# Loading p once in fp32 and scoring all batches by 32-row pieces in a two-stage attention and token-mixing kernel

## The chip, the cores and the metric

The kernel runs on one core of a Trainium2 chip. The core has a matrix engine (TensorE, PE in the profile), a vector engine (VectorE, DVE), an activation engine (ScalarE, ACT), a general engine (GpSimd, POOL) and a queue engine (SyncE, SP). Each works through its own instruction queue in order; semaphores hold an instruction back until what it needs is there. Sixteen DMA engines move data between HBM and the core's memory (SBUF); results of matmuls land in a second memory (PSUM) of eight banks. SyncE and ScalarE issue DMAs through hardware queues, GpSimd through a software queue; in this kernel the loads that cast fp32 to bf16 are all issued by GpSimd. The metric is device time in microseconds, as the median of several runs.

## What is computed

All inputs are fp32. There are 8 batches, 8 heads, 576 positions and a head size of 64; p has 32 packed positions per head.

```python
def sm_attn(qq, kk, vv):
    s = scale * np.matmul(qq, kk.transpose(0, 1, 3, 2))
    a = softmax(s)                      # over the last axis
    return np.matmul(a, vv)

p_packed = sm_attn(p, k, v)             # first attention: 32 x 576 scores per head
attn     = sm_attn(q, p_packed, p_packed)   # second attention: 576 x 32 scores per head
x   = attn.transpose(0, 2, 1, 3).reshape(8, 576, 512)
wq, wk = x @ w_q, x @ w_k               # 512 -> 64 each
mixed  = (wq @ wk.T / 8) @ x            # per batch
out    = np.maximum(mixed, 0) @ w_out   # 512 -> 512
```

## The kernel before

The program is one long list of steps, the string ORDER, that is read from left to right; each item issues the instructions of one step. `S1.3=2,3,6,7` is step S1 for batch 3 with PSUM banks 2, 3, 6 and 7; `X2.1.2@A` is step X2 for batch 1, part 2, on ScalarE (`@V` is VectorE, `@P` GpSimd, `@S` SyncE). So the order of each engine's queue is written out by hand, and batches overlap as the list interleaves them. A step waits only for what it needs, but it also waits for all that stands ahead of it in its engine's queue.

One batch goes through these steps:

- LD.k, LD.v, LD.q: loads, issued by GpSimd with a cast to bf16 (`load`, L153 to L185). Buffers for four batches (NL = 4) take turns. Half of k of batch 0 comes in fp32 by SyncE (LD.H) and is cast by ScalarE (HC).
- KT turns k by 32 x 32 blocks on VectorE (L242, `blocks`), S1 multiplies it with p on PE, X1 takes the exponential on ScalarE. In batches 2 to 7 S1 works by pieces of 32 rows (32 matmuls, L288) straight from pT, the turned p; X1 then comes in two parts (L299) and TE turns the result back (two VectorE instructions). In batches of DIAG (0 and 1) S1 works with a block-diagonal copy of p, `pblk` (36 matmuls, L278), X1 is one instruction (L296), and TE is not needed.
- PV multiplies with v (L321); RC and PP divide by the row sums (L325, L329); PT turns the packed result; QK multiplies it with the projection weights (L342), QKE and QD copy that out.
- QV turns q; S2 scores q against the packed result (L379), X2 takes the exponential (L384), RS and RR sum and invert (L400, L405), AM multiplies (L411) on VectorE or GpSimd; AT turns the result on PE (L420, L425), AE copies it out.
- WKQ, WE, GM, GE, Y, YE, MX, MR, RL, RLR are the token mixing up to the ReLU (L447 to L511); OT multiplies with the output weights (L546), OE and OEF copy out, ST and STF store.

p reaches the core twice: LD.E0 (ScalarE's queue) and LD.E1 (SyncE's) fetch batches 0 and 1 in fp32 with rows of 256 bytes, EC casts them on ScalarE, EX turns them, and four PB copies put them into `pblk`, which SET.pz0 has zeroed. LD.P0 to LD.P3 fetch all of p with a cast through GpSimd's queue, and PX turns it into pT later.

WARM items are filler: matmuls on a constant tile whose results nobody reads (L621). `WARM.15=3` is 15 units of 128 columns, in matmuls of 512 columns if not said otherwise (`WARM.16.128` is 16 units in matmuls of 128). Each shows as two instructions in the profile. HOLD.v7 is a tiny DMA on SyncE that reads the last v buffer, so that the stores behind it in SyncE's queue start only when that load has landed.

GpSimd's loads share eight completion semaphores in turn, so the issue of a load waits until the load eight places earlier has landed.

Of the kernel before, what the change touches and what calls it, by code (L numbers as in the profile page):

```python
# [7 lines left out]
NL, NB, NO, NE = 4, 3, 6, 2  # L8
DIAG = (0,1)
# [7 lines left out]
SET.v1@P S2.0.0=2,3 X2.0.0@A LD.v1 LD.P0 WARM.8=4 QK.0=4 RR.0.1@V AM.0.1@V QKE.0@A LD.q1 RS.0.0@V SET.aff@P  # L17
SET.idb@V WARM.3=5 S1.1=0,1,2 X1.1.0@A WARM.6=5 PV.1.0=4,5 PV.1.1 X2.0.2@A RR.0.0@V AT.0.1=3 AM.0.0@V AT.0.0=2
AE.0.0@A RC.1@V PP.1.1@V RS.0.2@V RR.0.2@V AM.0.2@V AE.0.1@A QD.0@A WARM.5=0 WKQ.0.0=0,1 AT.0.2=5 LD.k2
AE.0.2@A WARM.1=6 WKQ.0.2 LD.v2 WE.0.0@A WKQ.0.1 LD.q2 LD.k3 WE.0.1@A WARM.3=6 GM.0=5 PP.1.0@V PT.1@V QK.1=4  # L20
QV.1.2@V S2.1.1=6,7 GE.0@A S2.1.0=2,3 LD.O PX@V S2.1.2=0,1 KT.2.2@V QKE.1@A X2.1.1@A RS.1.1@V X2.1.0@A Y.0=4,5
YE.0@A WARM.1=6 S1.2=6,7,2,3 X2.1.2@A LD.v3 RS.1.0@V MX.0.1=4,5 RR.1.1@V X1.2.0@A TE.2.0@V X1.2.1@A TE.2.1@V
RR.1.0@V WARM.7=0 PV.2.0=0,1 PV.2.1 RL.0.1@A RS.1.2@V AM.1.0@V QD.1@A MR.0=6,7 RLR.0@A LD.k4 RR.1.2@V
MX.0.0=2,3 LD.q3 RC.2@V AT.1.0=4 AM.1.2@V AT.1.2=5 AE.1.2@A RL.0.0@A PP.2.1@V AM.1.1@P AT.1.1=6 AE.1.1@A
PP.2.0@V AE.1.0@V WARM.2=7 WKQ.1.0=0,1 WKQ.1.2 WARM.2=7 WKQ.1.1 QV.2.2@V WE.1.0@A PT.2@V S2.2.3=4,5 S2.2.2=2,3
KT.3.2@V WE.1.1@A GM.1=7 QK.2=6 GE.1@V WARM.3=0 Y.1=0,1 X2.2.2@A QKE.2@V S1.3=2,3,6,7 X2.2.3@A RS.2.4@V
RR.2.4@V LD.v4 X1.3.1@A TE.3.1@V X1.3.0@A TE.3.0@V OT.0.0=4,5 OT.0.1 LD.q4 YE.1@A AM.2.2@V OT.0.2=6,7 OE.0.0@V
OT.0.3 MR.1=2,3 OE.0.1@A RLR.1@V MX.1.1=0,1 PV.3.0=4,5 PV.3.1 RL.1.1@A RC.3@V PP.3.1@V PP.3.0@V KT.4.2@V
AM.2.3@P QD.2@P AT.2.3=2 AE.2.3@A OT.1.4=3 MX.1.0=6,7 AT.2.2=5 OEF.1.4@A AE.2.2@V WKQ.2.0=0,1 PT.3@V QV.3.2@V
WKQ.2.1 RL.1.0@A WKQ.2.2 WE.2.2@A S1.4=2,3,4,5 X1.4.1@A X1.4.0@A TE.4.1@V OT.1.0=6,7 LD.k5 GM.2=0 QK.3=1  # L30
QKE.3@A S2.3.2=4,5 X2.3.2@A S2.3.3=2,3 X2.3.3@A GE.2@V Y.2=0,1 OT.1.1 OE.1.0@A TE.4.0@V YE.2@V PV.4.0=4,5
PV.4.1 MX.2.0=0,1 RL.2.0@A RS.3.4@V LD.v5 RR.3.4@V RC.4@V LD.q5 PP.4.1@V PP.4.0@V PT.4@V OT.1.2=2,3 OT.1.3
QK.4=6 QV.4.2@V MX.2.1=0,1 MR.2=4,5 OE.1.1@A RL.2.1@A RLR.2@V AM.3.3@P QKE.4@V AT.3.3=7 AE.3.3@V QD.3@P
# [26 lines left out]
def kernel(  # L60
# [27 lines left out]
    P = 128  # L88
# [50 lines left out]
    def quarter(x):  # L139
        return slice(x * 32, (x + 1) * 32)  # L140
# [12 lines left out]
    def load(x, eng):  # L153
# [3 lines left out]
        elif a == "P":  # L157
            c = int(b)
            src = p.rearrange("b (i c) (y l) d -> c (b i) y (l d)", i=2, y=2)
            nc.gpsimd.dma_start(pbf[quarter(c)], src[c])  # L160
        elif a == "E":
            b = int(b)
            src = p[b].rearrange("(i c) l d -> (c l) i d", i=2)
            (nc.sync if eng == "S" else nc.scalar).dma_start(p32[:, 2 * b:2 * b + 2], src)
        elif a == "W":
            w = (moe_w_k, moe_w_q)[int(b)].rearrange("(i c j e) m -> (c j) i (e m)", i=2, c=4, e=2)
            nc.gpsimd.dma_start(wqk[:, :, int(b)].rearrange("a i e m -> a i (e m)"), w)
        elif a == "O":
            nc.gpsimd.dma_start(wout, moe_w_out.rearrange("(j a) n -> a j n", a=P))
        elif a == "H":  # L170
# [73 lines left out]
    def EC(eng, bk):  # L244
        copy(eng, pbe, p32.rearrange("a u d -> a (u d)"))
# [409 lines left out]
```

## Time and profile before

| | |
|---|---|
| median of 3 runs | 106.0 us (105.98 to 106.29) |
| profiled execution, whole | 105.18 us |
| its span, first to last instruction | 103.3 us |
| PE busy | 96.8 us, 94% of the span |
| PE weight loads | 58.4 us |
| VectorE busy | 75.7 us |
| ScalarE busy | 66.2 us |
| GpSimd busy | 49.9 us |
| bytes written by DMA | 25.16 MB |
| mean granted TensorE clock | 0.991 |

The busy time of PE includes the filler matmuls: 76 instructions of L621, 23.6 us with overlaps. The profile shows, for each group of instructions, its line, engine, operation and tiles, its count, its total and mean time, and what ended the idle time ahead of it. The chain of waits is followed back from the last instruction, at each step to what released it. A timeline row gives the start in us, the time in us, the engine, the line, the operation and in brackets the idle time before it. A row of a stretch of time (A:B) gives its length, then busy time and count of instructions of PE, PE weight loads, VectorE, ScalarE and GpSimd, the granted clock, the DMA engines' busy share, and GB/s written.

### The profile page before, as it was taken

To read this page: it belongs to the slowest core of one execution; us is meant where nothing else is said; L and a number is where in the kernel's file an instruction comes from. 1 tells how busy PE (TensorE), PEld (TensorE's weight loads), DVE (VectorE), ACT (ScalarE), POOL (GpSimd) and SP (SyncE) were. 2 spreads that over 40 slices of the span, in tenths; PEclk is the share of its full clock that TensorE was granted. 3 is DMA by queue.
4 is the path that set the end of the run, shared out by engine and by line. 5 is a ranking of instruction groups with operands and counts; after the bars stand their busy time and mean duration, and the time that the engine had idled before them with its cause. 6 is when DMAs were issued, how large, how long until landed. Compare 5 with 4: busy or idle time off the path is not lost.

```text
span 103.3 us, 3603 instructions
## 1 busy us (share of the span) xinstructions
PE 96.8 (94%) x1544; PEld 58.4 (57%) x1544; DVE 75.7 (73%) x150; ACT 66.2 (64%) x109; POOL 49.9 (48%) x76
## 2 busy tenths in 40 slices
PE   5999999999999999799999999999999999999950
PEld 3897545766756654456636655683567654744430
DVE  5072381969989899798699979989988999526310
ACT  5142104246896954779869869899898695659440
POOL 5779882962263316930049689506589129000000
PEclk9999999999999999999999999999999999999996
DMA  2999999999999999999999999999999999999884
GB/s 71 262 149 191 209 208 198 210 211 213 204 213 212 203 208 213 212 206 211 211 210 208 220 208 203 215 211 207 209 259 377 402 410 400 403 409 366 341 305 164
DMA packets 14079, 25.16 MB, mean 244 GB/s; under 512 B 2160, under 2 KB 7024, under 8 KB 14064
## 3 DMA queue, kind: packets, MB, share of 16 engines
q0 software_dynamic: 10448, 16.88, 85.1%
q1 hardware_dynamic: 3200, 7.87, 19.9%
q8 instruction: 12, 0.20, 0.7%
q10 hardware_dynamic: 416, 0.20, 0.7%
q14 instruction: 3, 0.02, 0.1%
HBM read 30.28 MB, written 9.44 MB: 384 GB/s over the span
## 4 chain that ended last, share of the span: by engine, by line
PE 73%; DVE 9%; DMA 5%; ACT 5%; POOL 3%; issue 2%; DVEq 0%; POOLq 0%; ACTq 0%
PE ps L546 25%; PE ps L621 13%; PE ps L321 6%; DMA k_sb<-in_k_dram 5%; PE ps L379 5%; PE ps L452 4%; PE ps L498 4%; PE ps L425 4%; DVE rs L400 3%; ACT e L384 3%; PE ps L447 3%; PE ps L278 2%; PE ps L473 2%; PE ps L288 2%; PE ps L342 2%; POOL a L411 2%
## 5 line engine op out<-in xcount | busy, mean ns | idle before, releaser
L546 PE MATMUL ps<-wout,relu 128*128 128x512 bf16 x124 | 30.5, 380 | 0.0
L411 POOL TENSOR_TENSOR a<-e,rr 128x1024 bf16<-128x1024 f32 (+2 forms) x13 | 15.6, 1211 | 19.1 <-DVE rr L405 11.0
L621 PE MATMUL ps<-o 128*128 128x128 f32 (+3 forms) x76 | 23.6, 452 | 1.3 <-DVE o L134 1.2
L127 ACT ACTIVATE o<-ps 128x1024 f32<-128x1024 f32 (+2 forms) x17 | 15.0, 888 | 6.9 <-PE ps L546 6.3
L546 PEld LDWEIGHTS <-relu 128*128 128x128 bf16 x124 | 10.7, 98 | 12.3 <-issue 1.8
L621 PEld LDWEIGHTS ps<-o 128*128 128x128 f32 x76 | 12.7, 220 | 7.1 <-issue 4.9
L384 ACT ACTIVATE e<-ps 128x256 f32<-128x256 f32 (+2 forms) x19 | 11.3, 621 | 5.9 <-PE ps L379 5.5
L509 ACT ACTIVATE relu<-ps 128x1024 bf16<-128x1024 f32 (+1 forms) x14 | 12.7, 933 | 2.2 <-PE ps L498 1.1
L242 DVE STREAM_TRANSPOSE kT<-k_sb 128x1152 uint32<-128x1152 uint32 (+1 forms) x9 | 11.1, 1232 | 3.0 <-DMA k_sb<-in_k_dram 2.9
L176 POOL DMA_DIRECT2D v_sb<-in_v_dram x16 | 10.1, 637 | 6.4 <-PE ps L425 2.1
L242 DVE STREAM_TRANSPOSE qT<-q_sb 128x1152 uint32<-128x1152 uint32 (+1 forms) x10 | 11.2, 1119 | 0.7 <-DMA q_sb<-in_q_dram 0.7
L400 DVE TENSOR_REDUCE rs<-e 128x16 f32<-128x512 f32 (+2 forms) x13 | 10.9, 846 | 0.5 <-ACT e L384 0.4
L321 PE MATMUL ps<-v_sb,e 64*64 64x192 bf16 x288 | 7.5, 245 | 0.7 <-DVE o L131 0.7
L299 ACT ACTIVATE e1T<-ps 128x576 bf16<-128x576 f32 x12 | 7.2, 663 | 1.3 <-PE ps L288 1.2
L127 ACT ACTIVATE aT<-ps 128x128 bf16<-128x128 f32 (+2 forms) x11 | 5.3, 506 | 3.6 <-PE ps L425 2.1
L321 PEld LDWEIGHTS <-e 64*64 64x64 bf16 x288 | 6.0, 107 | 2.6 <-issue 0.9
L127 ACT ACTIVATE wkq<-ps 128x448 bf16<-128x448 f32 (+1 forms) x9 | 6.3, 713 | 1.7 <-PE ps L452 1.4
L452 PE MATMUL ps<-aT,pqk 128*128 128x256 bf16 (+1 forms) x48 | 6.8, 246 | 0.1
L379 PEld LDWEIGHTS <-qT 64*128 64x128 bf16 x320 | 5.5, 94 | 2.3 <-issue 0.7
L379 PE MATMUL ps<-ppT,qT 64*128 64x64 bf16 x320 | 6.6, 190 | 0.0
L179 POOL DMA_DIRECT2D k_sb<-in_k_dram x7 | 5.2, 745 | 2.7 <-ACT g L127 2.7
L447 PE MATMUL ps<-pqk,aT 128*128 128x64 bf16 x80 | 6.1, 194 | 0.1
(80 smaller groups left out, 143.2 us busy)
## 6 DMA issues: line engine op xcount, KB each, us to landing
v_sb<-in_v_dram POOLq DMA_DIRECT2D x16, 288.0 KB, 11.5
out_dram<-o SPq DMA_DIRECT2D x9, 512.0 KB, 6.6
k_sb<-in_k_dram POOLq DMA_DIRECT2D x7, 576.0 KB, 11.9
q_sb<-in_q_dram POOLq DMA_DIRECT2D x6, 576.0 KB, 15.4
out_dram<-o POOLq DMA_DIRECT2D x4, 512.0 KB, 7.4
out_dram<-o SPq DMA_DIRECT2D x5, 256.0 KB, 2.7
q_sb<-in_q_dram POOLq DMA_DIRECT2D x4, 288.0 KB, 9.7
out_dram<-orem SPq DMA_DIRECT2D x4, 256.0 KB, 5.7
```

The source lines that it names most:

```text
L127: nc.scalar.activation(o, i, COPY)
L176: nc.gpsimd.dma_start(v_bufs[b % NL][halves(i), 0:7:2], src)
L242: nc.vector.transpose(o, i)
L321: nc.tensor.matmul(T["pv", b][halves(cc), i], lhsT, rhs, start=n == 0, stop=n == R - 1, skip_group_check=True)
L379: nc.tensor.matmul(ps[:, y, t - t0, i], lhsT, rhs, start=e == 0, stop=e == 1)
L384: nc.scalar.activation(e2[:, t0:t1].rearrange("a t (i y n) -> a y (t i) n", i=2, y=2), T["s2", b, c].rearrange("a y t i n -> a y (t i) n") ...
L400: nc.vector.tensor_reduce(rs[:, t0 * H:t1 * H], src, axis=AX, op=ADD)
L411: e.tensor_tensor(a2[:, t0:t1].rearrange("a t i (u l) -> a (t i u) l", l=L), e2v(b, c), T["rr", b][:, t0 * H:t1 * H].to_broadcast((P, (t1 ...
L452: nc.tensor.matmul(o, pqk[:, i, Dl:], aT[:, i, c0:c1], start=i == 0, stop=i == 1)
L509: nc.scalar.activation(o, i, RELU)
L546: nc.tensor.matmul(ps, lhsT, wout[:, j, :], start=j == 0, stop=j == NJ - 1)
L621: nc.tensor.matmul(bank(int(bk), [w]), warm[:, 0:P], rhs, start=True, stop=True)
```

## The change

- LD.E0, LD.E1 and LD.P0 to LD.P3 are gone. One load, LD.N, brings all of p in fp32 by ScalarE's hardware queue, in 128 rows of 4 KB. NC casts it in two halves, one on ScalarE, one on VectorE, and PX turns each half into pT, all before the first score step. EC, EX, the four PB copies and SET.pz0 are gone.
- DIAG is empty: S1, X1 and TE of batches 0 and 1 work as in the others, by pieces.
- The order of all steps, their engines and their banks is new. All 19 AM steps and all 8 QD steps are on GpSimd (13 and 4 before). The loads behind p and k come as g (half of k of batch 0), v0, r0 and q0 (halves of q), the two projection weights, k1, k2, v1, q1, v2, q2, k3, output weights, k4, v3, q3, v4, q4, k5, q5, v5, k6, v6, q6, k7, r7, v7, q7; before, k7, v7, r7, q7 stood last, and the four loads of p stood among the first ones. The filler is 81 units instead of 82. One store moves from GpSimd to SyncE, behind HOLD.

```diff
-DIAG = (0,1)
+DIAG = ()
...
-SET.warm@V SET.v3@V SET.pz0@V LD.E0@A SET.tab@A SET.aT1@V LD.H@S LD.P3 LD.E1@S EC@A EX@V PB.0.1@V LD.g0
-SET.v0@P HC@A PB.0.3@V PB.0.2@V KT.0.0@V KT.0.1@V LD.v0 PB.0.0@P WARM.4=0 WARM.16.128=0 S1.0=0,1,2 X1.0.0@A WARM.6=3
-PV.0.0=4,5 PV.0.1 RC.0@V LD.q0 SET.mask@P SET.idf@V SET.aT0@V QV.0.1@V PP.0.0@V LD.P2 LD.r0 PP.0.1@V PT.0@V
-SET.v2@V LD.W0 QV.0.0@V WARM.15=3 S2.0.2=6,7 LD.k1 LD.W1 SET.aT2@V LD.P1 KT.1.2@V S2.0.1=0,1 X2.0.1@A RS.0.1@V
...
+LD.H@S SET.warm@V SET.v0@V SET.aT0@V SET.aT1@V SET.aT2@V SET.idf@V LD.N@A SET.tab@A LD.g0 NC.0@A NC.1@V PX.1@V
+PX.0@V HC@A KT.0.0@V KT.0.1@V LD.v0 LD.r0 LD.q0 LD.W0 LD.W1 LD.k1 SET.mask@P SET.aff@P SET.idb@V WARM.4=0
+WARM.17.128=0 S1.0=0,1,2,3 X1.0.0@A TE.0.0@V X1.0.1@A TE.0.1@V WARM.8=4 PV.0.0=4,5 PV.0.1 RC.0@V PP.0.0@V
+PP.0.1@V PT.0@V QV.0.0@V QV.0.1@V WARM.12=6 S2.0.2=6,7 X2.0.2@A RS.0.2@V RR.0.2@V LD.k2 S2.0.0=0,1 X2.0.0@A
+S2.0.1=2,3 RS.0.0@V RR.0.0@V X2.0.1@A SET.v1@P LD.v1 LD.q1 RS.0.1@V SET.v2@P RR.0.1@V LD.v2 QK.0=4 QKE.0@A
+AM.0.2@P WARM.5=5 AT.0.2=5 AE.0.2@A AM.0.0@P WARM.5=6 AT.0.0=6 KT.1.2@V WARM.2=7 S1.1=0,1,2,3 AM.0.1@P
+AT.0.1=7 AE.0.0@V QD.0@P WKQ.0.0=4,5 WKQ.0.2 SET.v3@P X1.1.0@A LD.q2 LD.k3 WE.0.0@A LD.O AE.0.1@V KT.2.2@V
+LD.k4 WKQ.0.1 X1.1.1@A TE.1.1@V WARM.3=6 S1.2=0,1,6,7 LD.v3 WE.0.1@A GM.0=4 TE.1.0@V GE.0@A X1.2.0@A WARM.1=2
...
@@ load
-        elif a == "P":
-            c = int(b)
-            src = p.rearrange("b (i c) (y l) d -> c (b i) y (l d)", i=2, y=2)
-            nc.gpsimd.dma_start(pbf[quarter(c)], src[c])
-        elif a == "E":
-            b = int(b)
-            src = p[b].rearrange("(i c) l d -> (c l) i d", i=2)
-            (nc.sync if eng == "S" else nc.scalar).dma_start(p32[:, 2 * b:2 * b + 2], src)
+        elif a == "N":
+            src = p.rearrange("b (i c) (y l) d -> (c y) (b i) (l d)", i=2, y=2)
+            (nc.sync if eng == "S" else nc.scalar).dma_start(p32, src)
...
-    p32 = T["o"][NO - 1].rearrange("a t n -> a (t n)")[:, 0:4 * Dh].rearrange("a (u d) -> a u d", u=4)
+    p32 = T["o"][NO - 1].rearrange("a t n -> a (t n)")[:, 0:L * Dh // 2]
...
-    def EC(eng, bk):
-        copy(eng, pbe, p32.rearrange("a u d -> a (u d)"))
+    def NC(x, eng, bk):
+        n = L * Dh // 4
+        copy(eng, pbf[:, x * n:(x + 1) * n], p32[:, x * n:(x + 1) * n])
...
-    def EX(eng, bk):
-        blocks(pe.rearrange("a u l e -> a (u l e)").bitcast(u32), pbe.bitcast(u32))
-    def PX(eng, bk):
-        blocks(pT.rearrange("a u (y l) e -> a (u y l e)", y=2).bitcast(u32).rearrange("a (u l) -> a l u", l=L // 2),
-               pbf.bitcast(u32).rearrange("a (l n) -> a l n", l=L // 2))
+    def PX(x, eng, bk):
+        ls = slice(x * L // 4, (x + 1) * L // 4)
+        blocks(pT.rearrange("a u l e -> a (u l e)").bitcast(u32)
+               .rearrange("a (u y l) -> a l y u", y=2, l=L // 2)[:, ls],
+               pbf.bitcast(u32).rearrange("a (l y u) -> a l y u", l=L // 2, y=2)[:, ls])
```

More of the change, by code (lines that the diff above doesn't have):

```diff
@@ L17 @@
[L17 to L21, printed above, removed]
@@ new lines @@
+PV.2.0=6,7 PV.2.1 AM.1.2@P AT.1.2=0 AE.1.2@A RC.2@V AM.1.0@P WARM.4=1 AT.1.0=1 AE.1.0@A RR.1.1@V AM.1.1@P
+PP.2.1@V PP.2.0@V PT.2@V WARM.3=2 AT.1.1=2 QK.2=3 QV.2.2@V AE.1.1@A WKQ.1.0=4,5 QKE.2@V WKQ.1.2 WE.1.0@A LD.v4
+WKQ.1.1 WE.1.1@V S2.2.3=6,7 X2.2.3@A S2.2.2=0,1 GM.1=2 X2.2.2@A KT.3.2@V RS.2.4@V RR.2.4@V GE.1@A WARM.4=3
+Y.1=4,5 YE.1@A S1.3=6,7,0,1 X1.3.1@A MX.1.1=2,3 MX.1.0=4,5 OT.0.2=0,1 OT.0.3 X1.3.0@A RL.1.0@A OT.0.0=6,7
+RL.1.1@A TE.3.1@V OE.0.1@A AM.2.3@P AT.2.3=4 OT.0.1 KT.4.2@V AE.2.3@A TE.3.0@V AM.2.2@P AT.2.2=5 AE.2.2@A
@@ new lines @@
+HOLD.v7 ST.2.0@P ST.2.1@P RR.6.4@V AM.6.3@P X1.7.0@A OT.4.2=0,1 OT.4.3 TE.7.1@V MR.4=2,3 ST.0.0 QV.7.0@V
+QK.6=6 WE.5.2@A AM.6.2@P TE.7.0@V RLR.4@V OE.4.1@A GM.5=7 QV.7.1@V AT.6.3=4 AT.6.2=5 AE.6.2@V GE.5@A Y.5=2,3
+ST.1.4 QKE.6@A QD.6@P PV.7.0=0,1 PV.7.1 YE.5@V MR.5=6,7 MX.5.1=2,3 AE.6.3@A WKQ.6.0=4,5 WKQ.6.2 ST.3.4 RLR.5@A
+RC.7@V PP.7.1@V RL.5.1@A WKQ.6.1 PP.7.0@V ST.3.0 PT.7@V MX.5.0=6,7 RL.5.0@V ST.4.0 S2.7.0=0,1 OT.5.4=2
+OEF.5.4@V WE.6.2@A GM.6=3 ST.3.1@P S2.7.2=4,5 X2.7.0@A GE.6@A RS.7.0@V X2.7.2@A RS.7.2@V S2.7.1=0,1 X2.7.1@A
@@ L596, in STF @@
         q.dma_start(orows(b)[:, :, t * D:(t + 1) * D], T["o", b][:, t])
-    steps = dict(EC=EC, HC=HC, EX=EX, PX=PX, PB=PB, KT=KT, S1=S1, X1=X1, TE=TE, PV=PV, RC=RC, PP=PP,
+    steps = dict(NC=NC, HC=HC, PX=PX, PB=PB, KT=KT, S1=S1, X1=X1, TE=TE, PV=PV, RC=RC, PP=PP,
                  PT=PT, QK=QK, QKE=QKE, QD=QD, QV=QV, S2=S2, X2=X2, HA=HA, RS=RS, RR=RR, AM=AM,
```

63 lines of the change are left out of this document (26 added, 37 removed).

## The prediction

> **What bounds the kernel now.** I read the page's slices first.
>
> ```profile
> span 103.3 us, 3603 instructions
> PE   5999999999999999799999999999999999999950
> DMA  2999999999999999999999999999999999999884
> GB/s 71 262 149 191 209 208 198 210 211 213 204 213 212 203 208 213 212 206 211 211 210 208 220 208 203 215 211 207 209 259 377 402 410 400 403 409 366 341 305 164
> HBM read 30.28 MB, written 9.44 MB: 384 GB/s over the span
> ```
>
> Two resources are full almost from the first slice to the last: TensorE (PE) and the DMA engines. GB/s counts bytes written, so a load that casts fp32 to bf16 shows half of what it reads: the level of 210 up to slice 29 is 420 read, the same rate as the 400 of the fp32 stores behind it. The second view is the chain of waits, in order of time.
>
> ```profile
> 2.03 5.55 DMA k_sb<-in_k_dram
> ...
> 8.44 1.23 PE ps L278 x35
> 9.67 1.49 PE ps L621 x4
> 11.16 0.87 PE ps L321 x36
> 12.02 3.42 PE ps L621 x8
> ...
> 19.26 1.16 PE ps L278 x31
> ...
> 40.24 1.66 DVE a L411
> 41.89 1.14 DVE o L131
> ...
> 43.08 0.94 PE ps L321 x36
> ...
> 46.71 0.41 PE ps L288 x20
> ```
>
> Up to 8.4 us it is loads and transposes. From there PE's queue runs nearly without a gap, but not all of it is work: L621 are filler matmuls (WARM), which PE must finish before its next real step. The order has 82 units of filler (a unit is 128 columns), 20 of them ahead of the first score step. Behind 43.08 the chain is PE but for a few detours, to 99.5 (PE is busy for 4.47 us of the stretch from 95 on that is shown further down). So the end is: start of the first score step, plus PE's queue (work and filler), plus its stalls, and the transfers must keep up.
>
> **The change, part by part.** The sum is made against the profiled execution (105.18 us, span 103.3, so 1.88 outside the span); the median of the runs, 106.0, lies 0.82 above it.
>
> *Scores of batches 0 and 1.* Gone are two diagonal score steps of 36 matmuls, 1.23 and 1.16 us on the chain; in their place come two piece steps of 32, which the chain has at 0.41 (46.71 above) and, for batch 2 at 29.03, at 0.47. Gain 2.39 - 2 x 0.44 = **1.5 us** of PE queue; bounds 1.45 and 1.57.
>
> *Filler.* 82 units become 81, 21 of them ahead of the first score step, so 60 instead of 62 behind it. Fifteen units took 3.42 us (12.02), 0.228 each: **0.46 us** less. The extra unit ahead of the first score is one of the narrow ones; the row for 16 narrow and 4 wide ones is 6.98 us, so it adds some 0.4 and PE is free for the first score at about 8.18 + 0.4 = 8.58.
>
> *The start.* Before, ScalarE casts batch 0 and 1 of p, then the first half of k; VectorE turns both:
>
> ```profile
> o<-in_k_dram SPq DMA_DIRECT2D x1, 576.0 KB, 3.6
> 0.75 0.39 SPq L171 DMA_DIRECT2D o<-in_k_dram  x1
> 1.20 6.98 PE L621 MATMUL ps<-o 128*128 128x512 f32 x34 [1.20 <-DVE o L134]
> 4.90 0.42 ACT L127 ACTIVATE o<-o 128x256 bf16<-128x256 f32 x1 [2.16 <-DMA o<-in_p_dram]
> 5.22 1.15 ACT L127 ACTIVATE k_sb<-o 128x1152 bf16<-128x1152 f32 x1
> 5.73 0.44 POOL L129 COPY o<-o 32x256 bf16<-32x256 bf16 x1 [1.00 <-DVE o L242]
> 7.61 0.78 DVE L242 STREAM_TRANSPOSE kT<-k_sb 128x576 uint32<-128x576 uint32 x1 [0.32 <-DMA k_sb<-in_k_dram]
> L242 DVE STREAM_TRANSPOSE pT<-o 128x512 uint32<-128x512 uint32 x1 | 1.0, 1010 | 0.0
> 1.00:2.00 1.00, 0.80 (x1) 0.50 (x2) 0.88 (x3) 0.75 (x1) 0.67 (x1) 1.00 0.33 51
> 2.00:3.00 1.00, 1.00 (x2) 0.34 (x1) 0.37 (x3) 0.73 (x2) 1.00 (x3) 1.00 0.67 264
> 3.00:4.00 1.00, 1.00 (x6) 0.93 (x5) 0.00 (x0) 0.00 (x0) 0.70 (x2) 1.00 1.06 359
> 4.00:5.00 1.00, 1.00 (x7) 1.00 (x7) 0.00 (x0) 0.10 (x1) 0.72 (x2) 1.00 1.10 166
> 5.00:8.00 3.00, 3.00 (x24) 2.98 (x23) 2.24 (x6) 1.37 (x2) 2.10 (x8) 1.00 0.96 152
> ```
>
> The last piece of p, queued behind half of k on SyncE, was there at 4.90: 0.72 MB of fp32 by hardware queues. Now 0.52 MB of p and 0.59 MB of k go together, 0.39 MB more. At 359 per us that is 1.1 us for the pair; p is the smaller of the two and I place its landing at 5.3. Bounds: 4.35, if only k's half is shared with (issue 0.75 plus the 3.6 us to landing in its row), and 6.7, if p, and both halves of k share in thirds (1.57 MB, of which 0.67 by 4.0, the rest at 332 read). From there: p's ScalarE half, 512 columns, lies between 0.42 (256) and 1.15 (1152), about 0.63; k's cast 1.15; two turns of 0.78; hand-overs 0.1. First score at 5.3 + 3.44 = 8.75 against 8.44: **+0.3**, bounds +0.14 (filler) and +1.7. Queued behind the new wait for p on ScalarE stands k's cast, and for it wait the turn of k on VectorE and PE, even where k itself has long landed. VectorE's cast of the other half of p and the two turns into pT (1.01 us for the whole in its row) lie beside ScalarE's 1.78 and cost nothing; were that cover gone, it would be some 1.5. k's other half is issued 0.7 us earlier on GpSimd, since it is first in its queue now, and is wanted only at 7.9.
>
> *Softmax of batch 0.* One exponential becomes two with two turns.
>
> ```profile
> L299 ACT ACTIVATE e1T<-ps 128x576 bf16<-128x576 f32 x12 | 7.2, 663 | 1.3 <-PE ps L288 1.2
> L242 DVE STREAM_TRANSPOSE e<-e1T 128x288 uint32<-128x288 uint32 x12 | 5.4, 463 | 0.9 <-ACT e1T L299 0.7
> L411 POOL TENSOR_TENSOR a<-e,rr 128x512 bf16<-128x512 f32 x3 | 3.1, 1041 | 4.6 <-DVE rr L405 4.6
> L411 DVE TENSOR_TENSOR a<-e,rr 128x512 bf16<-128x512 f32 x3 | 2.1, 687 | 0.1
> ```
>
> Score to p-times-v was 11.16 - 8.44 = 2.72; now 0.47 + 2 x 0.66 + 0.46 and hand-overs, 2.4. It is covered by eight units of filler (1.8) either way: **0**; without them it would be 0.3 gained.
>
> *Normalising (AM) moves to GpSimd*, all 19 of them; six of them ran on VectorE. Each costs 0.35 more (1041 against 687 ns). So do the four copies of pqk (QD) that ScalarE and VectorE had; the rest of the queue behind each is loads. Beside fillers of 5, 5 and 2 units in batch 0 and 4, 4 and 3 in batch 1 most is hidden; I take **+0.5**, bounds 0 and 6 x 0.35 = 2.1.
>
> One stall goes. At 40.16 VectorE's AM on 256 columns took 1.73 us, where its likes at 24.08 and 32.56 took 0.43 and 0.41, and ended 0.3 us behind GpSimd's AM of batch 2:
>
> ```profile
> 39.70 1.90 POOL L411 TENSOR_TENSOR a<-e,rr 128x1024 bf16<-128x1024 f32 x1 [3.11 <-DVE rr L405]
> 40.16 1.73 DVE L411 TENSOR_TENSOR a<-e,rr 128x256 bf16<-128x256 f32 x1
> PE ps L321 <- DVE o L131: 0.7, 1, 0.7
> ```
>
> VectorE's next instruction let PE idle 0.7 us before 43.08. With no AM on VectorE the pair can't meet: **-0.7**, bounds -0.7 and 0 (late next: the 0.6 us AM queued behind the first on GpSimd). The Trainium skill, SBUF — State Buffer, section "SBUF: two separate sides", says that GpSimd and a VectorE instruction with two SBUF inputs lock each other out of a shared port for the whole instruction. The trace agrees (1.73 for 0.43). By that rule alone the next VectorE instruction would come 1.3 us sooner, of which the sum takes 0.7.
>
> PE's side: +0.3 - 1.5 - 0.46 + 0.5 - 0.7 = **-1.9 us**.
>
> *Transfers.* Two small loads of p (0.13 MB, 256-byte rows) go and none is added: 0.3 us at 420 read per us. The full loads are issued earlier, since GpSimd's queue is no longer held by a block copy (5.73) and by four loads of p; the low stretch 5 to 8 us (152 where 209 is usual) has 0.8 us to give. At the end:
>
> ```profile
> 90.00:95.00 5.00, 5.00 (x48) 2.29 (x45) 2.02 (x4) 3.80 (x7) 0.00 (x0) 1.00 0.97 385
> 95.00:101.00 6.00, 4.47 (x25) 2.23 (x23) 1.86 (x4) 2.85 (x6) 0.00 (x0) 1.00 0.88 334
> ```
>
> From 90 to 101 us 3.93 MB were written; at 405 this takes 9.7, so 1.3 us of slack. In all the transfers could end 2.4 us earlier if no gap were left, hardly more than PE's 1.9. Stores on SyncE wait (HOLD) for the last v, which now follows one half of q instead of preceding both; as loads or stores fill the engines then either way, I count nothing for it, nor for the one GpSimd store that moves to SyncE behind HOLD. I take **+0.4** back, bounds 0 and 1.6 (all of PE's 1.9 but the 0.3 of bytes). Sum -1.5: span 101.8, this execution 103.7, median 106.0 - 1.5 = **104.5**. Its own range is 103.5 to 105.4, set by the start and the AM.
>
> **The rivals.**
>
> *p comes late.* Three streams share in thirds, p lands at 6.7 and the first score starts at 10.15, 1.4 later than in the sum: -0.5, **105.5**. For it: all three are issued within 0.6 us. Against it: in the rows up to 5.00 all queues wrote 0.84 MB, 0.72 of it the hardware queues', so GpSimd's loads had moved 0.12. The Trainium skill, DMA: Bandwidth & Descriptors, "Queues, rings and completion order", has each DMA engine serve its rings in turn, a packet each. By that rule p would land with k; the trace bears it out only weakly.
>
> *The transfers bind.* PE gets 1.9 us ahead and then waits for loads or for stores, so only the 0.3 us of bytes remains: **105.7**. For it: 384 GB/s over the span. Against it: from 44 us on no load stands on the chain.
>
> *GpSimd's queue holds the AMs, and it gets slower.* GpSimd issues the loads too, and an issue waits there for an older load to land:
>
> ```profile
> wqk<-in_moe_w_k_dram POOLq DMA_DIRECT2D x1, 64.0 KB, 5.9
> 18.15 1.25 POOL L176 DMA_DIRECT2D v_sb<-in_v_dram  x2 [2.01 <-DMA k_sb<-in_k_dram]
> 24.55 0.62 POOL L176 DMA_DIRECT2D v_sb<-in_v_dram  x1 [1.71 <-DMA q_sb<-in_q_dram]
> ```
>
> In the new order the AMs of batch 0 stand behind the loads k2, v1, q1, v2, those of batch 1 behind q2, k3, the output weights, k4, v3, q3, those of batch 3 behind q5, v5, k6, v6. Behind each AM stands PE, which turns its result next. Two waits of 2.0 and 1.7 that reach the AMs in full cost 3.7: -1.9 + 3.7 = +1.8, **107.8**; it decides from 1.9 us on. For it: both rows fall in a stretch in which VectorE still did all AMs, so before they held back no AM. Against it: the last wait ahead of batch 0's AMs is for the first weight load, 5.9 us to landing in its row; by the durations of the issues ahead of it (0.56 to 1.24) it is issued some 4 us earlier than at 8.57 before, and no AM is wanted before p times v (to 12.0) and twelve filler units (2.7) are over.
>
> **How the numbers follow.** Forecast 0.55; p late 0.12; transfers bind 0.12; GpSimd's queue 0.21. About 0.3%, 0.3 us, is what can be told from no change. Faster: 0.53 of the forecast, 0.07 of late p, 0.06 of the transfers, together 0.66; the same: 0.02, 0.03 and 0.06, 0.11; slower: all of GpSimd's 0.21 and 0.02 of late p, 0.23. The range reaches from the forecast's low end, 103.4, into the GpSimd case, 107.0; above it stays half of that case, 0.1, and below it 0.08.
>
> **What would show it.** The first L281 matmul (the new file's line of the piece scores) at 8.6 to 9.0, with k's cast right behind p's; late p shows as ScalarE waiting on in_p beyond 6. AM of batch 0 with a VectorE reciprocal as its releaser: right; with a DMA issue just in front: the GpSimd rival. PE's last matmul near 97.6 instead of 99.5, and DMA share above 0.95 to the end, confirm the sum with its take-back. Wrong it is if PE gains fillers' worth of new idle time in 12 to 36 us, or waits there on k, q or v.

## The result, and the profile after

The change makes the kernel slower: 111.27 us median (110.54 to 112.02, 5 runs) against 106.0 (105.92 to 107.06), ratio 1.048 [1.041, 1.055]. The forecast was 104.5, in a range up to 107.0. The execution profiled after took 111.63 us, its span 109.9. Ratios, here and below, leave disturbed (slow) runs out, so that they can differ from the quotient of two medians.

First the slices of the page of the changed kernel:

```profile
span 109.9 us, 3565 instructions
...
PE   5980199999999999999989998996999999999950
PEclk9999557999999999999999999999999999999999
DMA  3699999999999999999999999999899955996695
GB/s 119 216 180 181 193 203 211 210 204 192 176 211 204 205 208 206 210 199 188 211 212 205 213 210 208 212 212 205 163 370 390 362 215 212 406 407 252 273 378 178
...
HBM read 30.15 MB, written 9.44 MB: 360 GB/s over the span
```

A slice is 2.75 us. TensorE idles in the fourth and most of the fifth (digits 0 and 1), and its granted clock is about half in the fifth and sixth, where it was full before. At the end the stores no longer fill the engines (215, 212, 252, 273 where 410, 400, 366, 341 stood before): outputs come late. The chain of waits (start, time, what) says what the idle time waits for:

```profile
0.74 9.95 DMA o<-in_p_dram
...
10.71 0.63 ACT o L127
11.34 1.06 ACT k_sb L127
...
12.42 1.45 DVE kT L235 x2
...
13.92 0.70 PE ps L281 x25
14.62 3.67 PE ps L614 x4
18.29 0.87 PE ps L314 x36
19.16 2.77 PE ps L614 x6
21.93 0.71 PE ps L372 x40
```

The single load of p lands at 10.7 us, and everything up to the first score hangs on it: first score 13.92 (8.44 before), p times v 18.29 (11.16), first second-stage score 21.93 (15.44). Of the 7.1 us by which p times v is late, the first score already has 5.5. The rest is the clock: the first scores and the eight units of filler behind them take 0.70 + 3.67 us here, and 0.47 + 1.92 at full clock (in the flat load's kernel below). That is 2.0 more, less the 0.3 by which the piece scores are shorter than the old ones. At the second stage 6.5 us are left, since three units of filler fewer stand in between. From there to the end of the span it is 109.9 - 21.93 = 88.0, before 103.3 - 15.44 = 87.9: the late start goes through to the end, and of what the change was to gain behind this point nothing shows in this kernel.

The stretches around it (PE, PE loads, VectorE, ScalarE and GpSimd busy with counts, clock, DMA share, GB/s written):

```profile
3.00:4.00 1.00, 1.00 (x6) 0.94 (x5) 0.00 (x0) 0.49 (x2) 1.00 (x3) 1.00 0.75 288
4.00:5.00 1.00, 1.00 (x9) 1.00 (x9) 0.00 (x0) 0.00 (x0) 1.00 (x2) 1.00 0.54 137
...
7.00:8.00 1.00, 0.69 (x7) 0.50 (x5) 0.00 (x0) 0.00 (x0) 0.65 (x4) 1.00 1.08 195
8.00:9.00 1.00, 0.00 (x0) 0.00 (x0) 0.00 (x0) 0.00 (x0) 0.00 (x0) 1.00 1.54 164
...
11.00:11.29 0.29, 0.00 (x0) 0.00 (x0) 0.26 (x2) 0.29 (x2) 0.00 (x0) 1.00 1.16 207
11.29:12.00 0.71, 0.00 (x0) 0.00 (x0) 0.71 (x2) 0.71 (x2) 0.68 (x1) 0.50 1.16 209
12.00:13.00 1.00, 0.00 (x0) 0.10 (x1) 0.82 (x2) 0.39 (x1) 0.70 (x3) 0.50 1.29 174
```

Two things stand there. Between 4 and 5 us the DMA engines are half idle although p is outstanding. And PE is empty from 7.7 us on; 3.6 us later, at 11.29, the clock falls in one step from full to half. The trace has it back at full at 18.12.

### The profile page after: what moved, and what is told of

The parts are those of the page before. It is cut to its first block, busy times and chain, and to the rows that moved or that the text cites. A ratio compares the mean times of both kernels' runs of the same rounds, so it can differ in the third digit from the quotient of the medians.

```text
span 109.9 us, 3565 instructions
## 1 busy us (share of the span) xinstructions
PE 95.5 (87%) x1519; PEld 56.1 (51%) x1534; DVE 71.6 (65%) x139; ACT 66.8 (61%) x112; POOL 53.2 (48%) x81
## 3 DMA queue, kind: packets, MB, share of 16 engines
HBM read 30.15 MB, written 9.44 MB: 360 GB/s over the span
## 4 chain that ended last, share of the span: by engine, by line
PE 69%; DMA 9%; DVE 9%; ACT 5%; issue 3%; POOL 2%; DVEq 0%; ACTq 0%; POOLq 0%
PE ps L539 24%; PE ps L614 13%; DMA o<-in_p_dram 9%; PE ps L314 5%; PE ps L372 5%; PE ps L418 4%; PE ps L281 3%; PE ps L445 3%; DVE kT L235 3%; PE ps L491 2%; PE ps L440 2%; PE ps L466 2%; POOL a L404 2%; ACT e L377 2%; PE ps L335 2%
## 5 line engine op out<-in xcount | busy, mean ns | idle before, releaser
L404 POOL TENSOR_TENSOR a<-e,rr 128x256 bf16<-128x256 f32 (+2 forms) x19 | 20.4, 1090 | 23.7 <-DVE rr L398 23.6
L539 PE MATMUL ps<-wout,relu 128*128 128x512 bf16 x112 | 29.2, 380 | 1.1 <-issue 0.5
L614 PE MATMUL ps<-o 128*128 128x128 f32 (+3 forms) x74 | 24.2, 468 | 1.3 <-DVE o L134 1.2
L127 ACT ACTIVATE o<-ps 128x1024 f32<-128x1024 f32 (+1 forms) x16 | 14.3, 892 | 4.2 <-PE ps L539 4.0
L614 PEld LDWEIGHTS ps<-o 128*128 128x128 f32 x74 | 12.0, 216 | 6.9 <-issue 4.9
L292 ACT ACTIVATE e1T<-ps 128x576 bf16<-128x576 f32 x16 | 9.7, 650 | 5.3 <-PE ps L281 5.1
L502 ACT ACTIVATE relu<-ps 128x1024 bf16<-128x1024 f32 (+1 forms) x13 | 12.1, 960 | 0.4 <-PE ps L497 0.3
L171 POOL DMA_DIRECT2D v_sb<-in_v_dram x16 | 10.1, 643 | 1.4 <-POOL v_sb L204 0.7
L281 PE MATMUL ps<-kT,pT 32*32 32x288 bf16 x256 | 4.5, 307 | 5.9 <-DVE kT L235 5.8
L235 DVE STREAM_TRANSPOSE e<-e1T 128x288 uint32<-128x288 uint32 x16 | 7.1, 454 | 1.9 <-ACT e1T L292 1.7
L131 DVE COPY o<-ps 128x1024 f32<-128x1024 f32 (+1 forms) x4 | 3.3, 822 | 5.4 <-PE ps L576 3.5
```

The source lines that it names most:

```text
L127: nc.scalar.activation(o, i, COPY)
L171: nc.gpsimd.dma_start(v_bufs[b % NL][halves(i), 0:7:2], src)
L235: nc.vector.transpose(o, i)
L292: nc.scalar.activation(e1T[:, x], T["s1", b][x].rearrange("a c m -> a m c"), EXP, scale=scale)
L404: e.tensor_tensor(a2[:, t0:t1].rearrange("a t i (u l) -> a (t i u) l", l=L), e2v(b, c), T["rr", b][:, t0 * H:t1 * H].to_broadcast((P, (t1 ...
L502: nc.scalar.activation(o, i, RELU)
```

## The experiments

Three theories stood against each other: the shape of the load (A), the company of GpSimd's loads (B), the ScalarE queue (C); with them, what the lost clock costs. A time without a ratio is that of a single run, unless a median is named.

### The same bytes in another shape

```diff
-            src = p.rearrange("b (i c) (y l) d -> (c y) (b i) (l d)", i=2, y=2)
+            src = p.rearrange("b h (y l) d -> (b h y) (l d)", y=2)
```

> The load of p reads its 128 rows of 4 KB in the order in which they lie in HBM (one outer dimension of 128 in the source instead of 8 by 16); bytes, row size, queue and all else stay. The rows land on other partitions, so the scores are taken with permuted rows of p and the output differs from the reference. Theory A (the load is given to only as many DMA engines as its outermost source dimension of 8 allows, so half of the 16 engines carry p beside their share of the other loads): with 128 it is spread over all, p lands by 6.0 us instead of 10.7, the first score starts by 9.4, PE does not lose its clock, and the time is 104 to 107 us. Theory B (p shares with the many loads that GpSimd now issues early, whatever its shape): p still lands behind 9 us and the time stays within 1 us of 111.3.

Measured: 104.76 us (104.59 to 104.85) against 106.11, ratio 0.990 [0.986, 0.994]. Its chain:

```profile
0.75 5.88 DMA o<-in_p_dram
...
9.86 0.47 PE ps L281 x19
10.33 1.92 PE ps L614 x4
12.25 0.87 PE ps L314 x36
13.12 2.77 PE ps L614 x6
15.89 0.71 PE ps L372 x40
```

The same 128 rows of 4 KB, by the same queue beside the same company, land 4.1 us earlier (at 6.6, where theory A had 6.0), and the kernel is 6.5 us faster. Its stretches from 3 to 5 us:

```profile
3.00:4.00 1.00, 1.00 (x6) 0.94 (x5) 0.00 (x0) 0.00 (x0) 1.00 (x3) 1.00 0.90 344
4.00:5.00 1.00, 1.00 (x7) 1.00 (x7) 0.00 (x0) 0.00 (x0) 1.00 (x2) 1.00 1.01 402
```

Where the changed kernel wrote 137 GB/s at half share, this one writes 402 at a full one. The issue took 0.40 us instead of 1.23. The queues' packets tell why; first the changed kernel, then this one, then one in which p goes by another queue (below):

```profile
q10 hardware_dynamic: 280, 0.66, 2.6%
```

```profile
q10 hardware_dynamic: 288, 0.66, 2.2%
```

```profile
q10 hardware_dynamic: 144, 0.13, 0.3%
```

Without p that queue has 144 packets, so the load has 136 in the first case and 144 in the second: 128 rows plus 8, and 128 rows plus 16. In the trace the extra packets have 4 bytes each, and the semaphore of p's load is raised 8 times between 9.69 and 10.69 us in the changed kernel, 16 times between 5.43 and 6.63 here. I read them as one completion for each DMA engine that takes part: 8 engines for the change's load, 16 for the flat one. The Trainium skill, DMA: Bandwidth & Descriptors, section "Why a DMA increments its semaphore by 16 and not by 1", gives the rule: a DMA is spread over the largest number up to 16 that divides the slowest dimension of both its patterns. The change's source has 8 there, (c y), the flat one 128; the trace agrees (8 and 16 packets).

The edit changes more than the number of engines: the rows come in the order of HBM, the issue is shorter, and p starts sooner. In the trace p's first row moves at 1.99 us here, beside those of k, whose last starts at 5.77. In the changed kernel it moves at 3.33, when k is nearly done (its last row starts at 3.63). GpSimd's first row moves at 4.9 to 5.0 in both kernels. By 5.0 us 410 of the flat load's 524 KB were written, and 229 of the change's.

### GpSimd's loads held back

Casting the second half of p on GpSimd holds every load behind it in that queue until p has landed. In the first of two kernels, GpSimd's half of k of batch 0 goes ahead of this, in the second it too stands behind.

```diff
-LD.N@A SET.tab@A LD.g0 NC.0@A NC.1@V PX.1@V
+LD.N@A SET.tab@A LD.g0 NC.0@A NC.1@P PX.1@V
```

> The cast of p's second half moves from VectorE to GpSimd, where it stands in front of all loads but the first half-load of k, so these are issued only when p has landed. p's access pattern keeps its outer 8. Theory A (half the engines, each with 64 KB of p beside k): p lands at 6 to 7.5, sooner than 10.7 as fewer loads share, but behind the 5.3 forecast. Theory B (sharing alone): p lands at 4.6 to 5.6. In both the later loads come some 4 us later than before; the time is no test.

Measured: 110.5 us; p lands at 9.35, later than either theory had placed it (7.5 at the latest).

```diff
-LD.N@A SET.tab@A LD.g0 NC.0@A NC.1@V PX.1@V
+LD.N@A SET.tab@A NC.0@A NC.1@P LD.g0 PX.1@V
```

> The changed kernel with all of GpSimd's loads behind p: the cast of p's second half moves to GpSimd and stands in front of them. Until p is there only p and SyncE's half of k are under way, so the rates written in this time are theirs. Theory A (half the engines carry p): once k's half has landed (about 4 us) p alone is written at 200 GB/s or less, half of the 400 that the stores reach, and it lands at 5.5 to 7.0. With all engines p would land by 4.7.

Measured: 111.75 us; p lands at 8.44, behind the 5.5 to 7.0 expected, while the rate came as expected, under 200 GB/s. From the chain and the stretches of this second kernel, in which only SyncE's half of k goes with p:

```profile
0.73 7.70 DMA o<-in_p_dram
```

```profile
5.00:6.00 1.00, 1.00 (x11) 1.00 (x10) 0.00 (x0) 0.00 (x0) 0.00 (x0) 1.00 0.49 119
6.00:7.00 1.00, 1.00 (x11) 1.00 (x10) 0.00 (x0) 0.00 (x0) 0.00 (x0) 1.00 0.53 131
```

With p alone in flight the engines are 0.49 to 0.53 busy and write 119 to 131 GB/s. Half of them, then, and less than a third of the 402 GB/s of the flat load's kernel (k and p together). GpSimd's loads together cost 10.7 - 8.4 = 2.3 us. So A and B both hold, and without B it would still be 8.4. But half the engines would explain half the rate, not a third: for the same busy share less was written too, 131 at 0.53, so 247 at a full one, against 398. Four loads on 16 engines, tried below without GpSimd's loads, show the same while p alone is in flight:

```profile
4.00:5.00 1.00, 1.00 (x7) 1.00 (x7) 0.00 (x0) 0.00 (x0) 0.00 (x0) 1.00 0.94 270
```

That is 287 at a full share, so this part doesn't come from the number of engines. Both kernels read rows that lie apart in HBM, the flat load reads them in order; this difference was not tried by itself.

Neither kernel gains more than 0.8 us in time: all later loads start late.

### The other hardware queue

```diff
-LD.H@S SET.warm@V ... SET.idf@V LD.N@A SET.tab@A LD.g0
+LD.N@S LD.H@S SET.warm@V ... SET.idf@V SET.tab@A LD.g0
```

> The same load of p is issued by SyncE ahead of its half of k instead of by ScalarE. Theory C (ScalarE's queue is late or slow: its issue took 1.23 us): p lands more than 2 us sooner than 10.7 and k's half stays near 4.4. Theories A and B: p lands within 1.5 us of 10.7, as shape and sharing are the same.

Measured: 114.5 us. p lands at 9.36 on SyncE's queue, 1.3 us sooner, and the half of k behind it only at 13.9 (the chain has it as 12.27 us of DMA from 1.63 on). C, which asked for more than 2 us, falls; and the load issued second in time is now the starved one.

### More filler ahead of the first score

```diff
-WARM.17.128=0 S1.0=0,1,2,3
+WARM.33.128=0 S1.0=0,1,2,3
```

> Sixteen more narrow filler units ahead of the first score, so that PE stays busy until p is there. If the idle stretch from 7.7 to 13.3 us cost PE its clock, the granted clock stays at 1.0, the eight filler units behind the first score take 1.8 instead of 3.7 us, p times v of batch 0 starts 2.0 sooner (16.2 to 16.6) and the time falls by 1.5 to 2.2 us to 109.1 to 109.8. If the clock doesn't matter for the end, it stays within 0.5 us of 111.3.

Measured: 110.09 us (109.41 to 110.96), ratio 1.039 [1.029, 1.050]. The chain of this kernel:

```profile
0.74 10.10 DMA o<-in_p_dram
...
14.07 0.48 PE ps L281 x23
14.55 1.91 PE ps L614 x4
16.46 0.87 PE ps L314 x32
```

p is as late as before, but the clock stays full, the filler takes 1.91 us again, and p times v starts 1.8 us earlier; at the end 111.27 - 110.09 = 1.2 are left of it. The intervals of the two ratios overlap, so this size is rough. About that much of the loss is the clock; the other 4 are the late start, less what the rest of the change gains.

### All engines, with the rows in their places

Eight loads of 16 rows, in turn on ScalarE's and SyncE's queues:

```diff
-            (nc.sync if eng == "S" else nc.scalar).dma_start(p32, src)
+            for z in range(8):
+                (nc.scalar, nc.sync)[z % 2].dma_start(p32[z * 16:(z + 1) * 16], src[z])
```

> p comes as in the change, on the same partitions, but as eight loads of 16 rows of 4 KB (outermost source dimension 16), in turn from ScalarE's and SyncE's queues, those of SyncE behind its half of k. Theory A (the number of engines follows from the outermost dimension): p lands between 6.0 and 7.5 us, as in the run that reads its rows in HBM order (6.6), the first score starts at 9.5 to 10.7, and the time is 104.4 to 105.6 us, below the kernel before. If instead rows that lie 32 KB apart in HBM are slow by themselves, p still lands behind 9 us and the time is above 109.

Measured: 111.34 us, ratio 1.054 [1.048, 1.059]: nothing gained. These are the numbers of the rival, slow rows, but a new wait stands in the way of reading them so. The chain has two loads of p one behind the other:

```profile
0.74 4.10 DMA o<-in_p_dram
...
4.86 6.08 DMA o<-in_p_dram
```

SyncE's last issue waited 2.3 us until ScalarE's first load of p had landed; issued at 4.86, it landed at 10.95. Four loads of 32 rows, two on each queue, avoid that wait (PX follows the other order of rows):

```diff
+            src = p.rearrange("b (i c) (y l) d -> c (b i) y (l d)", i=2, y=2)
+            for c in range(4):
+                (nc.scalar, nc.sync)[c % 2].dma_start(p32[quarter(c)], src[c])
...
```

> p comes as four loads of 32 rows, two from ScalarE's and two from SyncE's queue behind its half of k; the source's outermost dimension is 16 in each, and five loads leave hardware queues free of the wait that held the eighth of the eight loads back. Rows lie in another order in each group of 32 and the turn into pT takes that into account, so the computation is the reference's. Theory A (outermost dimension sets the number of engines): p lands between 6.0 and 7.5 us, the first score starts at 9.4 to 10.8 and the time is 104.4 to 105.4, faster than before by 0.3 to 1.2%. Theory F (rows 32 KB apart in HBM are slow whatever the number of engines, and loads of GpSimd that are under way by then starve them): p lands behind 9 and the time stays above 109.

Measured: 109.93 us, ratio 1.035 [1.031, 1.038]; the last of p lands at 9.3. Both are what theory F (slow rows, starved by GpSimd's loads) had expected, and not A: 16 engines by themselves don't bring p in time. And eight loads again, one of them issued by GpSimd ahead of its own:

```diff
-                (nc.scalar, nc.sync)[z % 2].dma_start(p32[z * 16:(z + 1) * 16], src[z])
+                eng = nc.gpsimd if z == 7 else (nc.scalar, nc.sync)[z % 2]
+                eng.dma_start(p32[z * 16:(z + 1) * 16], src[z])
```

> As the run with eight loads of 16 rows, but one of the eight is issued by GpSimd, ahead of its half of k, so that no load of p waits for an older one to be issued. Theory A: p lands between 6.0 and 7.5 and the time is near 105. Theory F: behind 9 and above 109.

Measured: 109.06 us, near F's numbers again; p lands at 8.89, the piece that ScalarE issued last, at 2.13. The four loads with all of GpSimd's loads held back (as above) fill the table below:

> The four hardware-queue loads of p of 32 rows (16 as the outermost dimension), with all of GpSimd's loads held behind p, as in the run that had the change's single load alone with half of k and saw it land at 8.4. If the number of engines is what made it slow there, p lands by 6.5 now; if a load whose rows lie in several dimensions is slow by itself, it lands behind 7.5 again. The time is no test, as all loads come later.

Measured: 110.02 us; p lands at 6.6, close to the 6.5 expected if the engines count. The last load of p in the chains of the four loads with company, then without:

```profile
1.94 7.36 DMA o<-in_p_dram
```

```profile
1.94 4.69 DMA o<-in_p_dram
```

| p lands at | with GpSimd's loads | without |
|---|---|---|
| one load, 8 engines | 10.7 | 8.4 |
| four loads, 16 engines | 9.3 | 6.6 |
| flat load, 16 engines | 6.6 | not tried |

So four loads on all engines, in two queues and with the rows in another order, are worth 1.4 to 1.8 us against the one on eight; the number of engines alone was not varied. The company is worth 2.3 to 2.7. The flat load is nearly through when GpSimd's rows begin to move at 4.93: 410 of its 524 KB are written by 5.0 us. Of the four loads' it is 176; their first row moves at 3.49, GpSimd's at 3.82. Why the first rows move so late is open. The flat load's issue was over at 1.15 us; of the others the last was over at 1.97 or later. That is a correlation; it was not tried by itself.

### p by GpSimd's queue

p in four cast loads ahead of all of GpSimd's others, without NC:

```diff
-LD.N@A SET.tab@A LD.g0 NC.0@A NC.1@V PX.1@V
-PX.0@V HC@A KT.0.0@V KT.0.1@V LD.v0
+LD.N SET.tab@A LD.g0 HC@A KT.0.0@V PX.1@V
+PX.0@V KT.0.1@V LD.v0
...
+            for c in range(4):
+                nc.gpsimd.dma_start(pbf[quarter(c)], src[c])
```

> p leaves the hardware queues: it comes as four loads of 32 rows with the cast to bf16, issued by GpSimd ahead of its half of k (as the loads of p in the kernel before, but all at the beginning); the two casts of p fall away, and the turn of k's first half goes ahead of the two turns of p. All else is the changed order. If p's late landing alone makes the change slow, p and GpSimd's half of k land by 8.5 us, since nothing on GpSimd's queue stands ahead of them, the first score starts at 9.3 to 10.2, and the time is 104.3 to 105.3, faster than before. If the order of the steps is slow by itself the time stays above 106.

Measured: 107.01 us, ratio 1.007 [1.003, 1.011]. p lands at 7.5, the first score starts at 10.1, only 0.25 behind the flat load, yet the kernel is some 1.8 us slower, above the 106 named for the case that the order of the steps is slow. Its chain shows where:

```profile
9.81 12.91 DMA k_sb<-in_k_dram
...
22.75 1.39 DVE kT L236
```

k of batch 2, a load that was not touched, stands behind the four loads of p, is issued at 9.81 instead of 8.54 and turned at 22.75 instead of 21.47: 1.3 us.

Then p by four loads on the hardware queues, and nothing else there: k of batch 0 goes whole through GpSimd.

```diff
-LD.H@S SET.warm@V ... LD.N@A SET.tab@A LD.g0 NC.0@A NC.1@V PX.1@V
-PX.0@V HC@A KT.0.0@V KT.0.1@V LD.v0
+SET.warm@V ... LD.N@A SET.tab@A LD.k0 NC.0@A NC.1@V PX.1@V
+PX.0@V KT.0.2@V LD.v0
```

> p in four loads of 32 rows by both hardware queues, each on 16 engines, and nothing else by hardware: k of batch 0 comes whole through GpSimd's queue, cast on the way, so the cast of half of k on ScalarE is gone too. Theory 'whatever of the hardware queues' loads has not landed when GpSimd's transfers come is starved': p now has about 1 MB and 4 us to itself, lands at 5.5 to 6.5, k of batch 0 at 8 to 9, the first score at 9.5 to 10.5, 104.0 to 105.5 us. Rival 'the early bytes bind, in whatever queue': the same 2.2 MB have to come before the first score, k lands at 10 or later, the first score at 11.5 or later, 106.5 us or more.

Measured: ratio 1.008 [1.003, 1.012], twelve runs from 106.02 to 109.12. Its chain:

```profile
1.51 7.57 DMA o<-in_p_dram
...
11.94 0.49 PE ps L282 x20
```

The rival's numbers came (the early bytes bind, in whatever queue): first score at 11.94, a time of 106.5 or more, and k at about 10, since GpSimd issues the load that waits for it at 10.00. But p, which has its own queues here, came late as well, at 9.1. From 3 to 4 us this kernel wrote 141 GB/s at a share of 0.92:

```profile
3.00:4.00 1.00, 1.00 (x6) 0.94 (x5) 0.00 (x0) 0.58 (x2) 1.00 (x3) 1.00 0.92 141
```

The flat load's kernel wrote 344 then. In the trace GpSimd's transfers, which begin at 3.1 us here, have more than half of the engines' busy time in this stretch and some three quarters from 4 us on, while p's last rows move at 7.8. None of the versions tried that place p as the change does is faster than the kernel before.

### The other terms: GpSimd's AM, the stall, the filler

The six AMs of batches 0 and 1 on VectorE (before the change five of them were there), once in the eight loads' kernel, once in the one with p by GpSimd:

```diff
-AM.0.2@P ... AM.0.0@P ... AM.0.1@P ... AM.1.2@P ... AM.1.0@P ... AM.1.1@P
+AM.0.2@V ... AM.0.0@V ... AM.0.1@V ... AM.1.2@V ... AM.1.0@V ... AM.1.1@V
```

> As the run with eight loads of p, but the six AM steps of batches 0 and 1 are on VectorE as before the change. The prediction put 0.5 us (0 to 2.1) on their move to GpSimd. If that is right the time falls by 0.3 to 1.0 against the run with eight loads; if VectorE is the fuller queue there (the turns of k and q of the next batches stand behind the AMs), it rises by 0.3 or more.

> As the run with p on GpSimd's queue, but the six AM steps of batches 0 and 1 are on VectorE as before the change. With eight loads of p this cost 1.4 us. If that holds with an early start too, the move of the AMs to GpSimd is a gain of 0.7 to 2 us and not the cost of 0.5 that the prediction took; if the loss came with the late start, the time stays within 0.5 of the run with the AMs on GpSimd.

Measured: a median of 112.70 us against the 111.34 of its neighbour, and ratio 1.017 [1.012, 1.021] against 1.007 [1.003, 1.011]. In the new order GpSimd is the better place for these, by 1.4 and 1.0 us. In the kernel before, only the AM of batch 2 moved (the stall of the prediction), then all six that VectorE had:

```diff
-AM.2.2@V
+AM.2.2@P
```

> The kernel before with one step moved: AM of batch 2's last tile from VectorE to GpSimd, where it stands ahead of the large AM of the same batch. The prediction put -0.7 us (-0.7 to 0) on the end of its 1.73 us stall. If the stall sat on the path, 0.4 to 0.7 us are gained; if it only moves the wait (the large AM comes 0.6 later on GpSimd), the time stays within 0.3.

> The kernel before with all six AM steps that VectorE had moved to GpSimd, its order and its start as they were. The moved AM of batch 2 alone was worth 0.5 us here; putting the AMs of batches 0 and 1 back onto VectorE cost 1.4 us in the order with the split load and 0.6 us in the one with p by GpSimd. If GpSimd is the better place whatever the order: 104.0 to 105.0 us. If the gain belongs to the new order, which leaves GpSimd free at those points (GpSimd here still has block copies and the loads of p in its queue): 105.3 to 107 us.

Measured: the one, 105.28 us against 105.62, ratio 0.995 [0.992, 0.998], faster than both kernels; all six, 110.87 against 105.85, ratio 1.048 [1.042, 1.054], far above both expectations. GpSimd's timeline of the latter (start, time, instruction, idle time before it):

```profile
14.01 0.52 POOL L160 DMA_DIRECT2D o<-in_p_dram  x1
21.24 1.04 POOL L411 TENSOR_TENSOR a<-e,rr 128x512 bf16<-128x512 f32 x1 [6.71 <-DVE rr L405]
22.24 0.76 POOL L185 DMA_DIRECT2D q_sb<-in_q_dram  x1
...
26.02 0.75 POOL L179 DMA_DIRECT2D k_sb<-in_k_dram  x1
```

The load of q of batch 1 stands behind an AM that waits 6.7 us for VectorE's reciprocal, that of k of batch 2 behind three. It is issued at 26.02 instead of 15.41 before, and the chain of this kernel goes through it. In the old order AMs hold up loads; in the new one the loads stand ahead of the AMs.

Last, the 40 units of filler behind the second-stage scores of batch 0, up to those of batch 2, left out of the eight loads' kernel:

```diff
-AM.0.2@P WARM.5=5 AT.0.2=5 AE.0.2@A AM.0.0@P WARM.5=6 AT.0.0=6 KT.1.2@V WARM.2=7 S1.1=0,1,2,3
+AM.0.2@P AT.0.2=5 AE.0.2@A AM.0.0@P AT.0.0=6 KT.1.2@V S1.1=0,1,2,3
...
```

> As the run with eight loads of p, without the 40 units of filler that stand behind the first S2 step. The prediction counted filler as 0.228 us of PE queue a unit, so 40 units would give 9.1. Theory D: filler stands in waits that other engines or loads set, so it is worth nearly nothing by itself: the time changes by less than 1 us if PE keeps its clock, and rises if the granted clock drops. Theory E (the sum's): at least 3 us are gained.

Measured: 112.33 us median, ratio 1.061 against the neighbour's 1.054. At 0.228 us a unit 9.1 us should have gone; none did. That they lie in waits is one reading; but without them the clock is lower as well (0.93 to 0.95 in these runs, 0.97 in the neighbour's), which takes time back, and the run does not part the two.

## Why the prediction was wrong, step by step

**What bounds the kernel.** "Start of the first score step, plus PE's queue, plus its stalls": the sum held, and its first term decided.

**The start** is the step that failed: +0.3 was forecast and +5.5 measured at the first score (+7.1 at p times v). p was placed at 5.3, "bounds 4.35 and 6.7"; it landed at 10.7. The first and the last divide bytes by rates that all sixteen engines reach, 359 and 332 per us, and 4.35 is the landing of k's half, a load on sixteen. The load of p had eight; its first row moved only at 3.33, behind nearly all of k's; and once GpSimd's transfers ran, from 5.0 on, its rate in the trace fell from 139 KB per us (4 to 5 us) to 70 to 72 (6 to 8 us). The upper bound did not bound: it gave p a full third, 111 KB per us. The prediction cited a rule (the Trainium skill, DMA: Bandwidth & Descriptors, section "Queues, rings and completion order": each engine serves its queues in turn, a packet each) by which p would land with k. In the two kernels' DMA issues (last column: us from issue to landing) the flat load's kernel agrees, 5.7 for k beside p's 5.88:

```profile
o<-in_k_dram SPq DMA_DIRECT2D x1, 576.0 KB, 5.7
```

The changed kernel does not, 3.6 beside 9.95:

```profile
o<-in_k_dram SPq DMA_DIRECT2D x1, 576.0 KB, 3.6
```

There p came behind k instead of beside it. The rule shares out an engine among loads that wait there; how many engines a load has, and when its rows are there to be served, it leaves open. The shape could have been read in the diff: (c y) in front is 8. With all engines on p (the flat load) it landed at 6.63, the late bound, and the first score began at 9.86.

Also missed: a queue that runs dry costs more than its idle time. The clock took about 1.2 us on top, and filler ahead of the first score, which the sum only counted as a cost (+0.4), gives it back.

**Scores.** Right: 0.47 on the chain of the flat load for the piece step of batch 0 and again for that of batch 1.

**Softmax of batch 0.** Right: 9.86 to 12.25 is 2.39, forecast 2.4.

**Filler.** Wrong in kind: a unit behind the first score isn't worth 0.228 us. Three units fewer between p times v and the second stage did shorten that stretch (3.42 to 2.77), as the chain shows, but 40 units further on were worth nothing on balance.

**AM on GpSimd.** Forecast +0.5 for longer instructions; putting those of two batches back costs 1.0 to 1.4 us, so GpSimd is a gain in this order and, for five of the same six, a loss of 5 in the old. The 0.35 us of an instruction was the wrong price; the place in two queues is what counts. The releaser is as the prediction said:

```profile
L404 POOL TENSOR_TENSOR a<-e,rr 128x256 bf16<-128x256 f32 (+2 forms) x19 | 20.4, 1090 | 23.7 <-DVE rr L398 23.6
```

Nearly all of GpSimd's idle time ahead of an AM ends with VectorE's reciprocal, none with a DMA, and so the rival "GpSimd's queue holds the AMs" did not come, though the time landed on its side.

**The stall.** -0.7 forecast, -0.5 measured (0.995 [0.992, 0.998]) when only that AM moves: right, somewhat oversized.

**Transfers.** The bytes are as forecast (read 30.15 MB for 30.28). They don't bind: the store slices have gaps. That the rest pays once p is in time is shown by the flat load, for that arrangement of rows: -1.1 us, 0.990 [0.986, 0.994], though it starts 1.1 later at the first score than forecast. Against the kernel before, its start is 1.4 later, so the parts behind the start gained 1.6 by the two spans (103.1 and 103.3) and 2.5 by the runs, where the forecast had 1.8 together. As a sum that is about right, partly by luck: the filler and the AM were mis-sized in opposite directions.

**The rivals.** "p comes late" named the right event, with a chance of 0.12, but not its mechanism: it had three streams share in thirds from the start. Its price, 105.5, was made from the same bound. It was not carried on to the clock.

**Open** stays why p's rows begin to move at 3.33 us in the changed kernel and at 1.99 in the flat one, why an engine moves fewer bytes where rows lie apart, and how much of the flat load's gain would remain with rows in their places.

## What to carry to other kernels

Before one load replaces several, look at the outermost dimension of its source and at what else is in flight: an early load that everything waits for wants all engines, and its rows moving before the bulk loads run. All engines alone did not do it here (four loads, 1.035). A time by bytes over full rate is a lower bound of a landing, not an estimate. And the engine of a step is chosen with its place in two queues: six AMs on GpSimd gained 1 us in one order and six, five of them the same, cost 5 in the other.

## What was not expected of the hardware

- A load on 8 of 16 engines, alone, moved 119 to 131 GB/s, less than a third of the 402 written by k and a flat load of p with all of them. Four loads of rows that lie apart, on all engines and alone, moved 270 at a share of 0.94. The issue of the first took 1.23 us, of the flat one 0.40.
- Hardware-queue loads beside GpSimd's casting loads fell far behind: 8.4 to 10.7 us, 6.6 to 9.3.
- 3.6 us after the last matmul the clock fell to half, for 6.8 us, so that some 4 us of the work that followed ran at half (filler of 1.9 us took 3.67). A pause of 2.9 us (k whole through GpSimd) left it full; in the kernel before with six AMs moved it fell after one of 1.5. So the length of one pause doesn't tell it.
- The issue of SyncE's last piece of p waited 2.3 us, to 4.86, for a load that ScalarE had issued.
